# Nine P tiles for six and one buffer of masked keys: P*V put off past the next tile's first score fills in a planned attention and GLU kernel

## The chip, the core and the metric

The kernel runs on one core of a Trainium2 chip. A core has five engines that run side by side, each with its own list of instructions: TensorE (PE in the profile; PEld is its weight load), VectorE (DVE), ScalarE (ACT), GpSimd (POOL) and SyncE (SP, which here only starts transfers). They meet at semaphores. The metric is device time of one execution in microseconds. Before the change it is 268.35 us, the median of three runs (267.51 to 268.49).

## The reference

```python
g = sigmoid((x * gate_w).sum(-1))               # one gate per token, x is [2048, 512]
q, k, v = heads(x @ wq), heads(x @ wk), heads(x @ wv)   # 32 heads of 16, 4 segments of 512 tokens
for s in range(4):
    p     = softmax(q_s k_s^T / 4 + causal mask)
    a_dot = p @ v_s
    a_mem = (phi(q_s) @ M) / (phi(q_s) @ z + 1e-6)       # phi(t) = t + 1 if t > 0 else exp(t)
    o_s   = sigmoid(beta) * a_mem + (1 - sigmoid(beta)) * a_dot
    M += phi(k_s)^T v_s;  z += sum(phi(k_s))
a = concat(o) @ wo
b = (gelu(x @ w_gate) * (x @ w_up)) @ w_down    # 512 -> 1792 -> 512
out = g * a + (1 - g) * b
```

Everything is bfloat16, with sums in float32.

## The kernel before

The program is a list of named tasks. A task is a few instructions on one engine (a few tasks may sit on ACT or DVE). The order of the tasks on each engine is written out in `ORDER` (lines 38 to 136), one string per engine; `schedule` merges the five lists, gives each accumulator of PSUM to the task that comes next, and `Emitter` puts in the semaphore waits that reads and writes of the same buffer need. So an engine's list is kept to the letter, and a task that is not ready holds up all that stand behind it.

The names, with `s` the segment and `t` one of four head tiles (eight heads each):

- `K`, `Q`, `V`: projections, full 128x128 matmuls of 512 columns, two per piece (line 498). Their results are copied out by ACT or DVE (`Kev`, `Qev`, `Vev`).
- `kp`: keys with every other head set to zero, into `kpad` (lines 719 and 728), one buffer for each parity `j`, double by segment before the change. `kl` is the same for the short rows along the diagonal.
- `qk{s}_{t}{A0,B0,L,A1,B1}`: score fills (line 859). Each writes all four score banks `X` with 8 tiled matmuls (`L` with 32). `exp` (ACT, line 866) reads all of `X` at once and writes one P tile `PT[slot]`; `msk` (POOL, line 870) sets the masked part to zero. `X` exists once, so the next fill waits for the exp. There are 72 fills, 64 of them into P tiles, handed out in turn by `pt_next % R_PT`.
- `pv{s}_{t}_{j}`: P*V (lines 909 and 917), 32 tiled matmuls into one accumulator. It reads the P tiles of one tile and parity, which then are free. `pvt` (DVE, line 924) transposes it into `Tb`, `norm` (lines 936 to 944) scales and transposes it back (through `ott`) into `oT`.
- `mz`: the product for M and z, 64 tiled matmuls. `pk`, `pq`: phi of keys and queries (an ACT exp and three DVE instructions); `pkT` and `oTd` are transposing transfers. `num`, `nump`: the memory read.
- `G`, `U`, `D`: gate, up and down projections, full matmuls; `D` ends with the output projection of the attention, which needs `oT`. `gelu` is on ACT, in a block of its own between the exps of two segments; `Um` (DVE, line 1009) multiplies. `fin` scales an output tile into one of `N_OST` buffers, and `out` stores it.

All full matmuls, `num`, `mz` and P*V share four PSUM accumulators `psW`; the next user of one waits until ACT or DVE has read it. What PE does between two score fills is mostly five pieces of two full matmuls; `pv` stands at some places among them.

SP starts the transfers: loads of x, weights, `Vlo` (copies of V rows), `pkT`, `oTd`, `out`, in the order of its list.

Of the kernel before, what the change touches and what calls it, by code (L numbers as in the profile page):

```python
# [17 lines left out]
H = 32  # L18
# [3 lines left out]
P = 128  # L22
ATT_SCALE = 0.25
EPS = 1e-6
R_PT = 6
N_W = 4
N_OST = 3
# [4 lines left out]
PATIENCE = 3.0  # L32
SWITCH = 0.097
COLD = 4.9
HOLD = 0.3
BLOCK, BLOCK_ASK, BLOCK_END = 256, 165, 208
OPEN_BONUS = 6.0
# [3 lines left out]
        "K0_2.0 K0_3.0 K0_0.1 K0_1.1 K0_2.1 K0_3.1 x0t0_1 x0t1_1 K0_0.2 K0_0.3 K0_2.2 K0_3.2 K0_2.3 K0_1.2 "  # L41
        "K0_1.3 K0_1.4 K0_1.5 K0_1.6 K0_1.7 K0_0.4 K0_0.5 K0_0.6 K0_0.7 K0_3.3 K0_2.4 K0_2.5 K0_2.6 K0_3.4 "
        "K0_3.5 Q0_2.0 Q0_1.0 Q0_1.2 Q0_2.2 Q0_3.0 K0_2.7 Q0_3.2 K0_3.6 Q0_0.0 Q0_0.2 K0_3.7 V0_1.0 V0_1.2 "
        "V0_0.0 V0_0.2 qk0_0A0 Q1_2.0 G0_6.0 V0_2.0 G0_6.2 V0_2.2 G0_1.0 qk0_0B0 G0_1.2 Q1_2.2 G0_4.0 G0_4.2 "
        "G1_5.0 G1_5.2 qk0_0L G1_7.0 V0_3.0 V0_3.2 G1_11.0 G1_11.2 G1_7.2 Q1_3.0 qk0_0A1 Q1_3.2 Q1_0.0 Q1_0.2 "
        "Q1_1.0 Q1_1.2 qk0_0B1 G1_3.0 G1_3.2 K1_2.0 G0_8.0 G0_8.2 K1_2.2 qk0_1A0 G1_2.0 G1_10.0 G1_2.2 G1_10.2 "
        "G0_5.0 G0_5.2 qk0_1B0 mz0 pv0_0_1 pv0_0_0 G1_12.0 qk0_1A1 K1_0.0 K1_0.2 G0_11.0 G0_11.2 K1_1.0 K1_1.2 "
        "qk0_1B1 G1_12.2 K1_3.0 K1_3.2 G0_12.0 G0_12.2 G0_10.0 G0_10.2 qk0_2A0 V1_1.0 V1_1.2 G1_4.0 G1_4.2 "
        "G0_9.0 qk0_2B0 pv0_1_1 pv0_1_0 G0_2.0 G0_2.2 G0_9.2 qk0_2L G0_7.0 G0_7.2 G1_6.0 num1_00.0 G1_6.2 G1_8.0 "
        "qk0_2A1 G1_8.2 G1_9.0 G1_9.2 G0_3.0 G0_3.2 qk0_2B1 V1_2.0 num1_01.0 Q2_2.0 V1_2.2 Q2_2.2 num1_02.0 "  # L50
        "qk0_3A0 V1_3.0 Q2_1.0 V1_3.2 G1_13.0 G1_13.2 Q2_1.2 qk0_3B0 pv0_2_0 pv0_2_1 G0_13.0 G0_13.2 num1_11.0 "
        "qk0_3A1 V1_0.0 V1_0.2 G0_0.0 G0_0.2 G1_1.0 G1_1.2 qk0_3B1 pv0_3_0 G1_0.0 G1_0.2 num1_10.0 Q2_3.0 Q2_3.2 "
        "U0_0.0 U0_0.2 qk1_0A0 pv0_3_1 U0_1.0 Q2_0.0 U0_1.2 Q2_0.2 U0_2.0 U0_2.2 U0_7.0 U0_8.0 U0_9.0 U0_9.2 "
        "U0_7.2 U0_8.2 U0_12.0 U0_12.2 U0_4.0 U0_4.2 U0_6.0 U0_6.2 U0_3.0 U0_3.2 U1_2.0 U1_2.2 U1_3.0 U1_3.2 "
        "U0_5.0 U1_5.0 U1_5.2 U0_13.0 U0_5.2 D0_0.0 D0_0.2 U0_13.2 num1_12.0 D0_0.4 D0_0.6 U0_11.0 U0_11.2 "
        "D0_0.8 U0_10.0 qk1_0B0 U0_10.2 D0_2.0 D0_2.2 D0_2.4 D0_2.6 qk1_0L D0_2.8 D0_2.10 D0_2.12 U1_4.0 U1_4.2 "
        "qk1_0A1 U1_0.0 U1_0.2 D0_2.14 D0_0.10 D0_2.16 D0_0.12 qk1_0B1 D0_0.14 U1_11.0 U1_11.2 U1_7.0 U1_7.2 "
        "K2_0.0 qk1_1A0 K2_0.2 U1_12.0 D0_0.16 U1_12.2 U1_10.0 qk1_1B0 U1_1.0 U1_10.2 U1_13.0 U1_1.2 U1_13.2 "
        "qk1_1A1 pv1_0_0 pv1_0_1 mz1 D0_3.0 D0_3.2 qk1_1B1 K2_2.0 D0_3.4 K2_2.2 D0_3.6 D0_3.8 qk1_2A0 V2_0.0 "
        "D0_3.10 pv1_1_0 pv1_1_1 qk1_2B0 D0_3.12 D0_3.14 V2_0.2 D0_3.16 K2_3.0 qk1_2L K2_3.2 D0_1.0 D0_1.2 "  # L60
        "D0_1.4 D0_1.6 qk1_2A1 V2_3.0 V2_3.2 D0_1.8 D0_1.10 U1_6.0 qk1_2B1 D0_1.12 D0_1.14 U1_9.0 U1_6.2 U1_9.2 "
        "qk1_3A0 K2_1.0 K2_1.2 Q3_0.0 Q3_0.2 D0_1.16 qk1_3B0 pv1_2_1 pv1_2_0 U1_8.0 U1_8.2 qk1_3A1 V2_2.0 V2_2.2 "
        "Q3_1.0 Q3_1.2 G2_2.0 qk1_3B1 G2_0.0 G2_0.2 V2_1.0 V2_1.2 G2_2.2 G2_1.0 G2_1.2 G2_3.0 G2_3.2 qk2_0A0 "
        "G2_5.0 G2_4.0 G2_4.2 G2_8.0 G2_8.2 G2_6.0 G2_5.2 G2_7.0 G2_6.2 G2_7.2 pv1_3_0 pv1_3_1 G2_9.0 G2_9.2 "
        "G2_10.0 G2_11.0 G2_10.2 num2_01.0 G2_11.2 G2_12.0 G2_12.2 G2_13.0 G2_13.2 Q3_2.0 Q3_2.2 num2_00.0 "
        "D1_0.0 U2_6.0 num2_02.0 D1_0.2 U2_6.2 D1_0.4 D1_0.6 D1_0.8 qk2_0B0 V3_3.0 D1_0.10 V3_3.2 U2_0.0 U2_0.2 "
        "D1_0.12 D1_0.14 qk2_0L Q3_3.0 Q3_3.2 V3_0.0 V3_0.2 D1_0.16 qk2_0A1 U2_8.0 U2_8.2 U2_13.0 num2_10.0 "
        "U2_13.2 U2_1.0 U2_1.2 qk2_0B1 U2_12.0 num2_11.0 U2_9.0 U2_9.2 D1_2.0 D1_2.2 qk2_1A0 D1_2.4 D1_2.6 "
        "num2_12.0 U2_4.0 U2_4.2 D1_2.8 qk2_1B0 D1_2.10 U2_12.2 D1_2.12 D1_2.14 D1_2.16 qk2_1A1 pv2_0_0 pv2_0_1 "
        "mz2 U2_3.0 U2_3.2 qk2_1B1 U2_10.0 K3_0.0 D1_3.0 K3_0.2 D1_3.2 qk2_2A0 U2_10.2 D1_3.4 K3_2.0 D1_3.6 "  # L70
        "D1_3.8 qk2_2B0 pv2_1_0 pv2_1_1 D1_3.10 D1_3.12 qk2_2L K3_2.2 D1_3.14 D1_3.16 K3_1.0 K3_1.2 qk2_2A1 "
        "V3_1.0 V3_1.2 D1_1.0 D1_1.2 D1_1.4 qk2_2B1 U2_5.0 U2_5.2 D1_1.6 D1_1.8 D1_1.10 qk2_3A0 U2_7.0 D1_1.12 "
        "U2_7.2 U2_11.0 U2_11.2 qk2_3B0 pv2_2_0 pv2_2_1 D1_1.14 D1_1.16 qk2_3A1 V3_2.0 K3_3.0 V3_2.2 K3_3.2 "
        "G3_0.0 qk2_3B1 G3_0.2 U2_2.0 G3_2.0 U2_2.2 G3_1.0 G3_1.2 G3_2.2 qk3_0A0 G3_3.0 G3_3.2 G3_4.0 G3_4.2 "
        "G3_6.0 G3_6.2 G3_5.0 G3_10.0 G3_5.2 G3_10.2 G3_7.0 G3_7.2 G3_9.0 G3_8.0 G3_8.2 G3_9.2 pv2_3_1 pv2_3_0 "
        "G3_11.0 G3_11.2 G3_12.0 G3_12.2 G3_13.0 G3_13.2 U3_12.0 U3_12.2 U3_7.0 U3_7.2 num3_00.0 D2_0.0 D2_0.2 "
# [26 lines left out]
    "dve": (
        "x0ev0a_0 x0ev0b_0 x0ev0_1 K0_1ev kl0_11 K0_0ev kp0_1 kl0_01 kl0_10 K0_2ev kp0_2 kl0_21 gmul0 kp0_0 "
# [101 lines left out]
class Sched:  # L206
# [6 lines left out]
    def add(self, task):  # L213
# [20 lines left out]
        if task.grp is not None:  # L234
            task.grp.left += 1
# [166 lines left out]
def mm_t(n):  # L402
    return max(0.026, n / 2370.0)
# [775 lines left out]
```

## Time and profile before

| | before |
|---|---|
| median of three runs | 268.35 us (267.51 to 268.49) |
| profiled execution, first to last instruction | 265.4 us (its total is not given apart) |
| PE busy | 261.5 us, 3021 matmuls |
| ACT busy | 210.6 us |
| DVE busy | 197.8 us |
| POOL busy | 105.4 us |
| score exp (ACT, line 866) | 72 of 1.88 us |
| granted TensorE clock | 1.00 |
| moved by DMA | 18.23 MB, 69 GB/s on average |

The profile gives one execution. Busy times of engines overlap. The chain of work that ended last is followed back from the last instruction, at each step to what released it or to what stood before it on its engine. A matmul's end in the trace is modelled, so consecutive matmuls overlap in it; from start to start is what one costs.

### The profile page before, as it was taken

Reading aid. Unit: us, or ns where it says so; the run is one execution under the profiler, and the core shown is the slowest. Engines: PE = TensorE matmul, PEld = TensorE weight load, DVE = VectorE, ACT = ScalarE, POOL = GpSimd, SP = SyncE. Lnnn points to the kernel's source line nnn. Section 1 sums busy time; section 2 is a strip of 40 time slices with the busy share of each in tenths; the row PEclk is TensorE's granted clock in tenths of the full one; section 3 lists DMA queues with packets and bytes.
Section 4 is the critical chain, followed back from the end, with each engine's and each line's share of the span. In section 5 each row is a group of like instructions: output and inputs, shape, how many; then the busy total and the mean of one; then the engine's idle time right before and its main releaser. Section 6 shows DMA issues by size and latency. Waiting matters only on the chain.

```text
span 265.4 us, 7149 instructions
## 1 busy us (share of the span) xinstructions
PE 261.5 (99%) x3021; PEld 119.0 (45%) x3021; DVE 197.8 (75%) x389; ACT 210.6 (79%) x187; POOL 105.4 (40%) x256
## 2 busy tenths in 40 slices
PE   8999999999999999999999999999999999999995
PEld 4644444444444435444344444443444444343452
DVE  1789869988988588886768968898685847694651
ACT  3699998999998898897957888867876886767712
POOL 8205777453101357173830161354173071436310
PEclk9999999999999999999999999999999999999999
DMA  7952223429510433200001433200000031300102
GB/s 231 323 161 51 54 82 83 140 42 308 161 51 0 100 77 70 80 0 2 2 0 21 101 84 78 82 2 22 2 2 0 2 78 29 77 22 2 42 0 82
DMA packets 32752, 18.23 MB, mean 69 GB/s; under 512 B 20560, under 2 KB 32720, under 8 KB 32720
## 3 DMA queue, kind: packets, MB, share of 16 engines
q1 hardware_dynamic: 31632, 16.73, 23.4%
q10 hardware_dynamic: 1088, 1.05, 1.1%
q8 instruction: 24, 0.39, 0.6%
q14 instruction: 8, 0.07, 0.1%
HBM read 9.84 MB, written 2.10 MB: 45 GB/s over the span
## 4 chain that ended last, share of the span: by engine, by line
PE 98%; ACT 1%; issue 0%; ACTq 0%
PE psW L498 76%; PE psXALL L859 9%; PE psW L909 6%; PE psXALL L498 3%; PE psW L917 1%; PE psW L583 1%; PE psW L825 1%; ACT pt L866 1%; PE psXALL L591 0%; ACT ost L1038 0%; ACTq L394 0%
## 5 line engine op out<-in xcount | busy, mean ns | idle before, releaser
L866 ACT ACTIVATE pt<-psXALL 128x2048 bf16<-128x2048 f32 x64 | 120.1, 1877 | 25.2 <-PE psXALL L859 20.1
L870 POOL TENSOR_SCALAR_AFFINE_SELECT pt<-pt 128x256 bf16<-128x256 bf16 x128 | 57.1, 455 | 106.7 <-ACT pt L866 102.1
L498 PE MATMUL psW<-xT,wu 128*128 128x512 bf16 x224 | 56.3, 380 | 0.0
L498 PE MATMUL psW<-xT,wg 128*128 128x512 bf16 x224 | 54.2, 380 | 0.0
L498 PE MATMUL psW<-wd,hT 128*128 128x512 bf16 x210 | 53.5, 380 | 0.0
L1009 DVE TENSOR_TENSOR hT<-psW,hT 128x512 bf16<-128x512 f32 x56 | 37.2, 685 | 18.6 <-PE psW L498 18.3
L870 POOL TENSOR_SCALAR_AFFINE_SELECT ptl<-ptl 128x512 bf16<-128x512 bf16 x32 | 23.0, 718 | 32.7 <-ACT ptl L866 31.1
L924 DVE STREAM_TRANSPOSE tb<-psW 128x512 f32<-128x512 f32 x32 | 21.5, 699 | 14.1 <-PE psW L917 14.1
L498 PEld LDWEIGHTS psW<-xT,wg 128*128 128x128 bf16 x224 | 20.4, 98 | 24.3 <-issue 1.5
L498 PEld LDWEIGHTS psW<-xT,wu 128*128 128x128 bf16 x224 | 20.2, 98 | 24.4 <-issue 2.7
L498 PEld LDWEIGHTS psW<-wd,hT 128*128 128x128 bf16 x210 | 19.2, 98 | 22.8 <-issue 2.1
L859 PE MATMUL psXALL<-qT,kpad 32*128 32x320 bf16 (+3 forms) x512 | 25.4, 273 | 0.2 <-ACT pt L866 0.2
L993 ACT ACTIVATE hT<-psW 128x512 bf16<-128x512 f32 x28 | 15.4, 600 | 8.0 <-PE psW L498 8.0
L859 PEld LDWEIGHTS psXALL<-qT,kpad 32*128 32x128 bf16 x512 | 7.6, 92 | 25.8 <-ACT pt L866 16.1
L909 PE MATMUL psW<-pt,vaug 128*17 128x192 bf16 (+3 forms) x512 | 18.8, 273 | 0.0
L866 ACT ACTIVATE ptl<-psXALL 128x2048 bf16<-128x2048 f32 x8 | 15.0, 1877 | 3.7 <-PE psXALL L859 3.7
L498 PE MATMUL psW<-xT,wk 128*128 128x512 bf16 (+1 forms) x80 | 17.8, 337 | 0.0
L498 PE MATMUL psW<-wv,xT 128*128 128x512 bf16 x64 | 17.3, 381 | 0.0
L498 PE MATMUL psW<-wo,oT 128*128 128x512 bf16 x60 | 16.4, 380 | 0.0
L768 POOL COPY exsT<-exs 32x4 f32<-32x4 f32 x64 | 13.4, 209 | 7.2 <-ACT exs L759 3.5
L909 PEld LDWEIGHTS psW<-pt,vaug 128*17 128x17 bf16 x512 | 10.3, 90 | 8.8 <-issue 3.0
L498 PE MATMUL psW<-xT,wq 128*128 128x512 bf16 x48 | 12.8, 380 | 0.0
(101 smaller groups left out, 308.1 us busy)
## 6 DMA issues: line engine op xcount, KB each, us to landing
out_dram<-ost SPq DMA_DIRECT2D x15, 128.0 KB, 1.7
wg<-in_B_w_gate_dram SPq DMA_DIRECT2D x2, 896.0 KB, 7.0
wu<-in_B_w_up_dram SPq DMA_DIRECT2D x2, 896.0 KB, 5.2
wd<-in_B_w_down_dram SPq DMA_DIRECT2D x2, 896.0 KB, 5.9
phkt<-in_A_x_dram SPq DMA_DIRECT2D x3, 512.0 KB, 4.4
vlow<-vaug SPq DMA_DIRECT2D x8, 136.0 KB, 2.6
wk<-in_A_wk_dram ACTq DMA_DIRECT2D x2, 256.0 KB, 4.2
hT<-in_A_x_dram SPq DMA_DIRECT2D x2, 256.0 KB, 3.9
```

The costliest lines, as they stand in the source:

```text
L498: return Instr(lambda e: e.matmul(view(), lhsT, rhs, start=first, stop=last), reads=reads, writes=[fkey if fkey is not None else g.key], e ...
L583: task(f"warm{i}", PE, [Instr(lambda e, gw=gw, n=n: e.matmul(gw.f32()[:, 0:n], ones[:, 0:128], ones[:, 0:n], start=True, stop=True), [], [ ...
L768: cross = task(f"exsT{s}", POOL, [Instr(lambda e, g=g, c=c: e.tensor_copy(exsT[sl][32 * g:32 * g + 32, c:16:4], exs[32 * c:32 * c + 32, s4 ...
L825: Instr(lambda e, t=t, kt=kt, c=c: e.matmul(gm.f32()[32 * c:32 * c + 32, 34 * t:34 * t + 34].rearrange("p (j e) -> p j e", e=17), phkt[:, ...
L859: instrs.append(Instr(lambda e, g=g, lhs=lhs, rhs=rhs, c0=c0, ncol=ncol: e.matmul(X[g][:, c0:c0 + ncol], lhs(32 * g), rhs(32 * g), start=T ...
L866: prev_exp[0] = exp_task(s, f"exp{s}_{t}{name}", [Instr(lambda e: e.activation(dst[:], XALL[:, :].rearrange("p (g c) -> p g c", g=4), ACTF ...
L870: task(f"msk{s}_{t}{name}", POOL, [Instr(lambda e, view=view, pat=pat, base=base: e.affine_select(out=view, in_=view, compare_op=ALU.is_ge ...
L909: instrs.append(Instr(lambda e, t=t, q=q, kb=kb, slot=slot, c0=c0: e.matmul(gp.f32()[32 * q:32 * q + 17, 128 * kb + 64:512], Vaug[sl][:, k ...
L917: instrs.append(Instr(lambda e, t=t, q=q, kb=kb, c0=c0: e.matmul(gp.f32()[32 * q:32 * q + 17, 128 * kb:128 * kb + 64], Vlow[j][:, kb, 4 * ...
L924: task(f"pvt{s}_{t}_{j}", DVE, [Instr(lambda e: e.transpose(Tb[:, j, :], gp.f32()[:, :]), [gp.key], [("Tb", j)], dve_t(512))], grp=gp)
L993: lambda e, g=g, ft=ft, s=s: e.activation(hT[s % 2][:, ft, :], g.f32()[:, :], ACTF.Gelu_apprx_tanh),
L1009: task(f"Um{s}_{ft}", DVE, [Instr(lambda e, g=g, ft=ft: e.tensor_tensor(hT[sl][:, ft, :], g.f32()[:, :], hT[sl][:, ft, :], ALU.mult), [g.k ...
```

## The change

Four things change in the program, and then all five orders are rebuilt.

- `R_PT` goes from 6 to 9: nine P tiles. The memory for them comes from `kpad`, now one buffer per parity instead of two, from `ott`, now the first part of `Tb`, from `gmat`, now `gexp`, and from `N_OST`, 2 output buffers instead of 3.
- `kp` of segments 1 to 3 becomes four tasks of two tiles each (names `kp{s}_{i}{j}`), since a half of `kpad` can be written once the fills of those two tiles are done.
- The P*V tasks stand later in PE's list, past the first fills of the next tile, and some directly between two fills. The most fills that are unread at once are nine.
- Five evacuations of the first x tiles all go to DVE. First use of a score bank by `Q0` is now ordered after the x transposes that used it (`held`). The rest in the planner's classes (`table`, `grps`, `patience`, `ahead`) only names things for the building of orders.

```diff
-R_PT = 6
+R_PT = 9
 N_W = 4
-N_OST = 3
+N_OST = 2
...
-    kpad = [[sb(f"kpad{j}_{i}", [P, 4, 512]) for i in range(2)] for j in range(2)]
+    kpad = [sb(f"kpad{j}", [P, 4, 512]) for j in range(2)]
...
-    ott = sb("ott", [P, 512])
+    ott = Tb.bitcast(BF)[:, 0:1, 0:512].rearrange("p a b -> p (a b)")
...
-    gmat = sb("gmat", [P, H], F32)
+    gmat = gexp
...
+        keys = [key, ("x0ps", 0)] if c0 == 512 else [key]
...
+        held = [("x0ps", c0) for c0 in ((0, 512), (1024,), (2048,), (3072,))[t]] if x else []
...
+        ins[0].writes += tuple(held)
...
         if s > 0:
-            for j in range(2):
-                task(f"kp{s}_{j}", DVE, [
-                    Instr(lambda e, j=j: e.tensor_scalar(kpad[j][sl][:], kT[:], maskc[j][:, 0:1], None, ALU.mult),
-                          [("kT", t) for t in range(4)] + [("c", "mask", j)],
-                          [("kpad", j, sl, t) for t in range(4)], 0.78)])
+            for i in range(2):
+                for j in range(2):
+                    task(f"kp{s}_{i}{j}", DVE, [Instr(lambda e, i=i, j=j: e.tensor_scalar(
+                        kpad[j][:, 2 * i:2 * i + 2, :], kT[:, 2 * i:2 * i + 2, :], maskc[j][:, 0:1], None, ALU.mult),
+                        [("kT", t) for t in (2 * i, 2 * i + 1)] + [("c", "mask", j)],
+                        [("kpad", j, t) for t in (2 * i, 2 * i + 1)], dve_t(1024, 4, ap=True))])
...
-                dst, dk = (oT[sl][:, t, :], ok) if s == 0 else (ott[:], [("ott",)])
+                dst, dk = (oT[sl][:, t, :], ok) if s == 0 else (ott, [("Tb", 0)])
```

PE's order in segment 1, from the third tile's first fill, and the last segment's fills around 225 us, before and after:

```diff
-qk1_1A1 pv1_0_0 pv1_0_1 mz1 D0_3.0 D0_3.2 qk1_1B1 K2_2.0 D0_3.4 K2_2.2 D0_3.6 D0_3.8 qk1_2A0 V2_0.0
-D0_3.10 pv1_1_0 pv1_1_1 qk1_2B0 D0_3.12 D0_3.14 V2_0.2 D0_3.16 K2_3.0 qk1_2L
+qk1_1A1 D0_2.8 num1_12.0 num1_10.0 num1_11.0 D0_2.10 D0_2.12 D0_2.14 qk1_1B1 D0_2.16 U1_12.0 U1_9.0 U1_9.2 U1_12.2
+qk1_2A0 pv1_0_0 pv1_0_1 pv1_1_1 mz1 pv1_1_0 qk1_2B0 D0_1.0 D0_1.2 D0_1.4 D0_1.6 D0_1.8 V2_3.0 qk1_2L
...
-qk2_1A1 pv2_0_0 pv2_0_1 mz2 U2_3.0 U2_3.2 qk2_1B1
+qk2_2A0 mz2 pv2_0_0 pv2_0_1 pv2_1_0 pv2_1_1 qk2_2B0
...
-qk3_1A1 U3_5.0 U3_5.2 num3_12.0 U3_0.0 U3_0.2 qk3_1B1
+qk3_1A1 U3_13.0 num3_11.0 U3_13.2 D2_1.8 D2_1.10 D2_1.12 num3_12.0 qk3_1B1
```

SP's order after the first `pkT`:

```diff
-pkT0_1 Vlo0_0 Vlo0_1 pkT0_2 pkT0_0 pkT0_3 xt1 x2_3 x2_2 x2_1 x2_0 w_wu0 oTd1_1 oTd1_0 w_wu1 w_wd1 w_wo Vlo1_1 w_wd0
+pkT0_0 pkT0_1 Vlo0_0 Vlo0_1 w_wu0 pkT0_3 pkT0_2 x2_3 xt1 w_wd0 w_wu1 x2_0 x2_2 x2_1 w_wd1 w_wo x3_1 oTd1_0 Vlo1_1
```

## The prediction

> **What bounds the kernel now.** I read the busy lines first: which engine has no room, and at what clock.
>
> ```profile
> PE 261.5 (99%) x3021; PEld 119.0 (45%) x3021; DVE 197.8 (75%) x389; ACT 210.6 (79%) x187; POOL 105.4 (40%) x256
> PEclk9999999999999999999999999999999999999999
> PE 98%; ACT 1%; issue 0%; ACTq 0%
> ```
>
> PE is busy 99% of a 265.4 us span, at the full granted clock in every slice, and the chain that ended last runs over PE for 98% of it. A busy PE can hide waits, so I read next the chain in order of time (start, length, what).
>
> ```profile
> 180.93 2.26 PE psW L498 x10
> 191.23 3.13 PE psW L498 x14
> 194.68 7.01 PE psW L498 x32
> ...
> 233.00 0.97 PE psW L498 x4
> 237.80 0.33 PE psXALL L859 x8
> 238.13 2.26 PE psW L498 x10
> 240.39 0.33 PE psXALL L859 x8
> ```
>
> Full matmuls cost 0.216 us each ((7.01-0.97)/28), and each piece has 0.10 to 0.11 us on top (0.97-4*0.216), whatever its length. That is the price of changing between full matmuls and the tiled ones of the score fills (L859) and P*V (L909, L917). Nothing else is in these pieces: PE issues back to back. I laid the start times of all PE instructions beside these prices; only 0.43 us in 261 is left over, and 0.24 of it is one place, in the timeline:
>
> ```profile
> 223.68 0.62 PE L909 MATMUL psW<-pt,vaug 128*17 128x448 bf16 x16
> ...
> 224.24 0.61 PE L909 MATMUL psW<-pt,vaug 128*17 128x448 bf16 x16
> ...
> 224.89 0.40 PE L859 MATMUL psXALL<-qT,kpad 32*128 32x448 bf16 x8
> ...
> 225.48 1.88 ACT L866 ACTIVATE pt<-psXALL 128x2048 bf16<-128x2048 f32 x1 [0.70 <-PE psXALL L859]
> ...
> 227.42 0.40 PE L859 MATMUL psXALL<-qT,kpad 32*128 32x320 bf16 x8 [0.17 <-ACT pt L866]
> ```
>
> Here a fill began at 224.89, its exp ran 225.48 to 227.37, and the next fill, which writes the same score banks, started at 227.42. So a round from fill to fill takes at least 2.53 us by ACT; the usual one (0.33+2.26) takes 2.59 by PE, 0.06 above it. This round had 2.27 us of PE work, and PE waited. The rows also price P*V: the second starts 0.56 us after the first, the fill 0.65 after that, so leaving P*V costs 0.09 to 0.10 as well, also towards a fill.
>
> The waits view says how near the others are:
>
> ```profile
> ACT pt L866 <- PE psXALL L859: 20.1, 38, 1.1
> PEld psXALL L859 <- ACT pt L866: 17.8, 42, 0.7
> DVE hT L1009 <- PE psW L498: 18.3, 25, 2.9
> PEld psW L498 <- DVE otok L800: 0.6, 3, 0.2
> ```
>
> ACT and DVE wait for PE; the weight loads' waits on ACT run under the preceding matmuls.
>
> **The change part by part.** No PE instruction is added or removed: 3021 before and after. What can move PE is its mode changes, its waits and the two ends.
>
> *Mode changes.* Counted along both PE orders, neighbours of different kind go from 165 to 159: full to tiled 75 to 71, P*V (or memory product) to full 15 to 9, P*V to fill 3 to 7, fill to P*V 12 to 10, fill to full 60 to 62. By the rows above each costs 0.10, towards a fill too: -6*0.10 = -0.6 us. Placing P*V between fills saves only the return to full matmuls, which is why the gain is not larger.
>
> *The wait at 225.4.* Adding up the new order's PE work from fill to fill with the rows' prices, that round now holds 2.91 us. Before, one round held 2.27 and ten 2.48 to 2.51; after, four hold 2.48 to 2.50. The wait goes: -0.24. The six fewer short rounds are worth at most 6*0.04 = 0.2 and the left-over is 0.19, so I take -0.1.
>
> *ACT work between exps.* Exp is 1.88 of the 2.53, so another ACT instruction of up to 0.65 (copies of 0.60, a 0.62 sum) fits a round free; a phi exp of 1.05 does not. The tightest place: phi exp and copy in two successive rounds, 1.88+1.05+1.88+0.60 = 5.41 of ACT in 5.53 of PE. It fits. If one such round fails it costs 0.1 to 0.4. I take 0, range 0 to 0.4.
>
> *P*V put off.* With nine P tiles up to nine fills stay unread: P*V of tiles 0 and 1 of the second segment follows the ninth. Each P*V drags two DVE transposes (0.70 each) and the normalisation (recip, scales, transpose, sum: about 2.6) with it; behind them on DVE stand the U products that free PE's four accumulators, and the output projection waits for the result. Cover: DVE idles 67 us in all, but the tightest place has none to spare: the projection piece of segment 2 that needs the last normalisation lies 5.5 us of PE work after its P*V begins, and P*V pair 1.2, 0.3 to the transpose (224.24 to 224.55 in the timeline), a transpose 0.70, a U product 0.69 that stands between, and normalisation 2.6 make 5.5. Accumulators change hands with less spare than before in more places, too. Before, loads waited about 1.4 us in total on DVE and none of it reached PE; bounds 0 to 1.4, I take +0.1, nearest to what reached PE.
>
> *One buffer of masked keys.* Per segment two 128x2048 scalings (0.78 each, six in all) become four of 128x1024. Rows: 128x512 takes 0.35, 128x2048 0.78, so about 0.49; DVE gains 3*(4*0.49-2*0.78) = 1.2 us, inside its idle time. The new wait is on the previous segment's fills of the same two tiles; each half stands in DVE's list after those fills, so what is queued behind it (U products) does not stall. 0; if one is late, a U product of 0.69 is late with it, 0 to 0.7.
>
> *Transposed result in Tb, gate matrix in the exponentials' place.* Readers and writers are on DVE in this order already, or long done: 0. *x0 score banks held:* the first Q matmul in each starts at 8.64 or later, the last x evacuation ended at 7.14: 0. All five evacuations of x go to DVE: the last then ends at 6.75+0.43 = 7.18, and its first reader starts at 7.33: 0, at most 0.1.
>
> *Two output buffers.* The last copy now waits for the landing of tile 1's store. From the end of tile 1's work to the last matmul's end the order holds 3.4 us of PE work; copy 0.75, landing 1.7 and 0.3 between make 2.75. 0; with the transposes' landing of 2.4 it would be just even.
>
> *SP order.* Three weight loads (wu0, wd0, wu1) move ahead of pieces of the next x. The nearest row: two such loads, issued at 58.9 and 59.5, landed at 63.9 and 66.3. Issued after the memory product at about 45, behind 512 KB of tokens, they land by about 53; the x transposes behind them by about 54. The Q matmul that reads them is at 56.8 on the new order. wg's second half is issued at 12.0, landed at 17.9 and is now read at 19.1 instead of 20.6. 0; 0 to 1.0 if a landing slips.
>
> *Instruction fetch.* The page shows no cost, only the queue:
>
> ```profile
> q8 instruction: 24, 0.39, 0.6%
> ```
>
> 24 packets for 6042 weight loads and matmuls: one per 256, that is per 128 matmuls. Densest before: memory product and one P*V pair, 128 matmuls; P*V pairs of two tiles and the memory product now form runs of 192, 2.87 us, in two places (segments 1 and 2). Within them 128 matmuls take 1.9 us. The trace's packets took 0.88 to 1.40 us and began at least 5.7 us apart. If asking and landing take the 1.6 us of the shortest row of transfers, nothing is lost; at the transposes' 2.4 to 2.8, 0.5 to 0.9 in each place. I take 0, the nearest case being the dense runs before, none of which stalled; range 0 to 1.8.
>
> [...]
>
> **Sum**: -0.6 - 0.24 - 0.1 + 0.1 = -0.84 us against the profiled execution, whose span is 265.4; 2.95 us of the median lie outside it and are untouched (the execution's own total is not given apart). 268.35 - 0.85 = 267.5 us, -0.3%. Three runs of before spread over 0.98 us, so 0.5% (1.34 us) is about what a measurement tells from no change.
>
> **The rivals.**
> *Nothing gets in the way and the small left-overs vanish too.* -0.6-0.43-0.1 = about -1.15, 267.2, and a median as low as before's lowest run against its median gives 266.4: faster by over 0.5%. For it: PE has hardly any wait left. Against: it needs luck in the runs.
> *The gain is given back on ACT or DVE.* PE's freed 0.1s fall in rounds 0.06 above ACT's floor, and accumulators are tighter. For it: 42 of the fills' weight loads waited on ACT. Against: those waits were hidden. Gives back 0.4 to 0.8: 268.1.
> *Slower: instruction fetch in the two runs of 192.* It decides from the point where two stalls exceed 0.84, a landing of 2.3 us; slower by over 0.5% from 0.84+1.34 = 2.18 in two places, a landing of 3.0. At 3.3 us it costs 2*1.4: 270.3. For it: the 512 KB token load is issued as the memory product ends, and those rows land in 4.4. Against: packets took 1.4 at most beside other traffic.
> *Slower by a late transfer*, x behind the weights: +1.0 to +2.5, about 269.
>
> **How the numbers follow.** Forecast 0.52 (own range 267.0 to 268.0), left-overs and luck 0.23, given back 0.12, fetch 0.08, late transfer 0.05. Faster by over 0.5%: 0.23 and 0.03 of the forecast's edge, 0.26. Slower: fetch and half of the late transfer, 0.11. Same: 0.63. The range leaves out the fetch and the low end of the luck: 266.5 to 269.2.
>
> **What would show it.** Right: PE work from first to last matmul shorter by 0.6 to 1.1 us, no wait at a fill over 0.1, P*V followed by a fill in seven places at 0.65 start to start. Wrong: a gap inside the runs of P*V and memory product with no releaser (fetch); weight loads waiting on DMA before a Q matmul; fills over 2.6 us apart with ACT as releaser.

## The result, and the profile after

The changed kernel takes 270.10 us (median of six executions, 269.42 to 273.52); the kernel before, run beside it and earlier, 267.67 us (six, 267.26 to 268.49). The ratio is 1.0087 with a 95% interval of 1.0058 to 1.0116: slower by 0.87%, where 0.3% faster was forecast and the range ended at 269.2. The slowest of the six, 273.52, ran at a mean granted clock of 0.994 and is not in the ratio, nor are the slowest execution of `e1_split` (275.79) and of `e5_shift48` (276.0) below; without it the median is 269.94. The profiled execution took 270.25 us, its span is 268.5 us; before's was 265.4.

The page of the kernel after, first the busy time of the engines, then the queue that brings the instructions (packets, MB, share) and the chain that ended last by engine:

```profile
PE 262.4 (98%) x3021; PEld 119.2 (44%) x3021; DVE 202.2 (75%) x399; ACT 210.5 (78%) x180; POOL 105.1 (39%) x256
...
q8 instruction: 23, 0.38, 0.6%
...
PE 90%; DMA 5%; SPq 2%; ACT 1%; issue 1%; ACTq 1%
```

PE's share of the chain fell from 98% to 90%, although PE has the same 3021 matmuls. What has come in is DMA and SP's queue, where the chain runs back through a transfer that PE waited for, and 1% "issue", time that nothing in the profile explains. The waits view of PE (engine, line, what it waited for: us in total, times, longest) names them:

```profile
PE psXALL L860 <- issue: 1.3, 1, 1.3
...
PE psW L497 <- DMA xT<-in_A_x_dram: 0.5, 1, 0.5
PE psXALL L497 <- DMA wq<-in_A_wq_dram: 0.4, 1, 0.4
```

The timeline of PE around 109 us shows the largest (start, length, instruction, idle time before it):

```profile
105.30 0.40 PE L860 MATMUL psXALL<-qT,kpad 32*128 32x448 bf16 x8
105.63 0.61 PE L908 MATMUL psW<-pt,vaug 128*17 128x448 bf16 x16
...
107.52 0.81 PE L828 MATMUL psW<-vaug,phkt 128*32 128x34 bf16 x64
...
108.83 0.31 PE L860 MATMUL psXALL<-qT,kpad 32*128 32x320 bf16 x3
110.42 0.39 PE L860 MATMUL psXALL<-qT,kpad 32*128 32x320 bf16 x5 [1.28 <-issue]
```

This is the run `qk1_2A0 pv1_0 pv1_1 mz1 qk1_2B0` that the prediction priced. PE stops in the middle of one fill, with three of its eight matmuls done. No semaphore can stand there: the other five read and write the same buffers. From start to start the stop costs 1.58 us. A second one, 0.31 us, follows the same run in segment 2 (the chain, followed in order of time, has "174.89 0.15 issue" there).

The chain in order of time shows the second loss:

```profile
50.30 3.20 SPq L524
...
53.55 4.78 DMA xT<-in_A_x_dram
58.33 0.05 issue
58.38 0.82 PE psW L497 x3
```

The transposing load of a quarter of x for segment 2 is issued at 53.55 and lands at 58.33; the second matmul of `Q2_2` waits for it: 0.65 us from start to start.

The place around 225 us that the prediction gave 0.24 for is clean. The two rounds that begin with the exps below are 2.89 us (227.02 to 229.91) and 2.6 us long, and ACT waits for PE, not PE for ACT (ACT's timeline; in brackets ACT's idle time and what ended it):

```profile
227.02 1.88 ACT L866 ACTIVATE pt<-psXALL 128x2048 bf16<-128x2048 f32 x1 [0.96 <-PE psXALL L860]
229.91 1.88 ACT L866 ACTIVATE pt<-psXALL 128x2048 bf16<-128x2048 f32 x1 [1.01 <-PE psXALL L860]
```

I laid all PE start times of the two traces beside the same price for each kind of piece and neighbour. PE's work went from 260.32 to 259.70 us, PE's waits (what is over those prices) from 0.55 to 4.30. The terms of the 3.16 us between the two spans:

| term | predicted | in the two profiles |
|---|---|---|
| mode changes, 165 to 159 | -0.6 | -0.62 |
| wait at 225.4 | -0.24 | -0.24 |
| instruction fetch, two runs | 0 | +1.58 + 0.31 |
| SP order, x behind weights | 0 | +0.65 |
| P*V put off, accumulators | +0.1 | +0.20 |
| a fill that waits for an exp, at 47.7 | 0 | +0.09 |
| small left-overs, shorter rounds | -0.1 | none found |
| two output buffers | 0 | +0.21 |
| the head: warm-up matmuls, load of wq | not in the sum | +0.4 + 0.60 |

The last row is not the change's. The warm-up matmuls ran at 0.43 us each until 3.4 us in before's profile and until 4.5 in the one after, and wq's second half landed at 9.27 and at 10.45, from the same list of transfers. In the kernels below with the head of after the wait for wq was 0 to 0.22, and `e7_bmodes`, whose head is that of before to the instruction, also did its first transposes at 4.85 us, not 4.34. The first transposes in before, in after and in `e7_bmodes` (PE's timelines):

```profile
4.34 0.62 PE L591 MATMUL psXALL<-ident,hT 128*128 128x128 bf16 x8
4.75 0.61 PE L591 MATMUL psXALL<-ident,hT 128*128 128x128 bf16 x8
4.85 1.06 PE L591 MATMUL psXALL<-ident,hT 128*128 128x128 bf16 x8
```

So before's one profile had a fast start. Without the last row the terms add up to 2.18, and the medians differ by 2.27 (269.94 less 267.67), not by 3.16.

### The profile page after: what moved, and what is told of

The parts are those of the page before. It is cut to its first block, busy times and chain, and to the rows that moved or that the text cites. A ratio compares the mean times of both kernels' runs of the same rounds, so it can differ in the third digit from the quotient of the medians.

```text
span 268.5 us, 7155 instructions
## 1 busy us (share of the span) xinstructions
PE 262.4 (98%) x3021; PEld 119.2 (44%) x3021; DVE 202.2 (75%) x399; ACT 210.5 (78%) x180; POOL 105.1 (39%) x256
## 3 DMA queue, kind: packets, MB, share of 16 engines
q10 hardware_dynamic: 1088, 1.05, 1.2%
## 4 chain that ended last, share of the span: by engine, by line
PE 90%; DMA 5%; SPq 2%; ACT 1%; issue 1%; ACTq 1%
PE psW L497 71%; PE psXALL L860 9%; PE psW L908 6%; DMA wq<-in_A_wq_dram 3%; PE psXALL L497 3%; DMA xT<-in_A_x_dram 2%; SPq L524 2%; PE psW L916 1%; ACT ptl L866 1%; ACTq L528 1%; PE psW L828 0%; SPq L528 0%; ACT ost L1036 0%; ACT hT L511 0%; ACTq L393 0%
## 5 line engine op out<-in xcount | busy, mean ns | idle before, releaser
L869 POOL TENSOR_SCALAR_AFFINE_SELECT pt<-pt 128x256 bf16<-128x256 bf16 x128 | 55.3, 443 | 111.9 <-ACT pt L866 107.0
L497 PE MATMUL psW<-wd,hT 128*128 128x512 bf16 x210 | 55.3, 380 | 0.0
L869 POOL TENSOR_SCALAR_AFFINE_SELECT ptl<-ptl 128x512 bf16<-128x512 bf16 x32 | 23.9, 746 | 29.1 <-ACT ptl L866 27.4
L497 PEld LDWEIGHTS psW<-wd,hT 128*128 128x128 bf16 x210 | 18.4, 98 | 21.2 <-issue 2.7
L771 POOL COPY exsT<-exs 32x4 f32<-32x4 f32 x64 | 15.4, 240 | 8.2 <-ACT exs L762 4.6
L497 PE MATMUL psW<-wv,xT 128*128 128x512 bf16 x64 | 18.1, 380 | 0.0
L514 DVE CAST hT<-psW 128x512 bf16<-128x512 f32 x20 | 13.5, 686 | 4.3 <-PE psW L497 4.3
```

The costliest lines, as they stand in the source:

```text
L497: return Instr(lambda e: e.matmul(view(), lhsT, rhs, start=first, stop=last), reads=reads, writes=[fkey if fkey is not None else g.key], e ...
L514: alts[DVE] = [Instr(lambda e: e.tensor_copy(dst(), src()), reads=reads, writes=writes, est=dve_t(n))]
L771: cross = task(f"exsT{s}", POOL, [Instr(lambda e, g=g, c=c: e.tensor_copy(exsT[sl][32 * g:32 * g + 32, c:16:4], exs[32 * c:32 * c + 32, s4 ...
L869: task(f"msk{s}_{t}{name}", POOL, [Instr(lambda e, view=view, pat=pat, base=base: e.affine_select(out=view, in_=view, compare_op=ALU.is_ge ...
```

## The experiments

### The two runs broken up, x first, and both

`e1_split` puts the second P*V pair behind full matmuls in both runs. `e2_xfirst` gives SP the x quarters ahead of the weights. `e3_both` has both edits.

```diff
 PE, e1_split
-qk1_2A0 pv1_0_0 pv1_0_1 pv1_1_1 mz1 pv1_1_0 qk1_2B0 D0_1.0 D0_1.2 ... D0_1.8 V2_3.0 qk1_2L
+qk1_2A0 pv1_0_0 pv1_0_1 mz1 D0_1.0 qk1_2B0 D0_1.2 ... D0_1.8 V2_3.0 pv1_1_1 pv1_1_0 qk1_2L
-qk2_2A0 mz2 pv2_0_0 pv2_0_1 pv2_1_0 pv2_1_1 qk2_2B0 D1_3.0 D1_1.0 ... D1_1.6 qk2_2L
+qk2_2A0 mz2 pv2_0_0 pv2_0_1 D1_3.0 qk2_2B0 D1_1.0 ... D1_1.6 pv2_1_0 pv2_1_1 qk2_2L
 SP, e2_xfirst
-x2_3 xt1 w_wd0 w_wu1 x2_0 x2_2 x2_1
+x2_3 x2_0 x2_2 x2_1 xt1 w_wd0 w_wu1
```

> The changed kernel with two edits of PE's order, all else kept: in segment 1 the second P*V pair (pv1_1) moves from inside the run qk1_2A0 .. qk1_2B0 to just ahead of qk1_2L, behind five full-size pieces, and one D piece goes between mz1 and qk1_2B0; in segment 2 the same with pv2_1 and mz2. The work is the same; the two runs of 192 small matmuls are broken into 144 or fewer with full-size pieces between. Theory A, instruction fetch: PE takes its instructions in blocks of 256 (128 matmuls with their weight loads), the next block but one is only asked for when a block is entered, and a block of small matmuls is through in 1.9 us (109 us) and 3.9 us (175 us, its stall within) while the ask takes about 3.5. With full-size pieces in it the block lasts over 4.5 us. Expected: the stall of 1.58 us at 109 and the one of about 0.3 to 0.5 us at 175 are gone, four more mode changes cost 0.4; time 270.1 - 1.9 + 0.4 = 268.6 us (268.2 to 269.0). Rival B, a late P tile, mask or PSUM bank at these two places that the profile does not name: the fill qk1_2B0 stands in the same place behind the same exponentials, so it stalls as before (1.3 to 1.6 us) and the time is 270.3 to 270.7 us.

> The changed kernel with one edit of SP's order: the last three quarters of x for segment 2 (x2_0, x2_2, x2_1) are issued ahead of xt1 and the two weight pieces w_wd0 and w_wu1, as far as before had them ahead. Theory: the wait of Q2_2.2 for x2_1 at 58.4 us (0.65 us with the slow start behind it) goes, since x2_1 lands about 8 us earlier; the weight pieces land by about 58 and are first read near 63 (U1) and 85 (D0), the gate input xt1 is read by DVE only near 60. Expected 270.1 - 0.6 = 269.5 us (269.2 to 269.8), the two stalls at 109 and 175 unchanged at 1.6 and 0.3 to 0.5 us. Rival: the wait is not on the path, because PE then waits as long a little later (for U weights or DVE): the 0.65 us are gone at 58 and come back before 70, 270.1 us.

> The edits of e1_split and e2_xfirst together. If the two stalls of instruction fetch and the wait for x2_1 are separate terms, they add: 270.1 - 1.9 + 0.4 - 0.6 = 268.0 us (267.5 to 268.5), level with the kernel before (267.67). If the gains overlap or the time is lost again somewhere else, over 268.6 us. If something beyond these two makes the changed kernel slow (more work on PE by the new order, contention of ACT or DVE), it stays above 269 us.

Measured against before (267.85 us in these runs): `e1_split` 269.29 us (269.08 without its slowest execution), ratio 1.0043 (1.0019 to 1.0068); `e2_xfirst` 269.24 us, 1.0047 (1.0016 to 1.0078); `e3_both` 268.66 us, 1.0022 (1.0003 to 1.0040).

In `e1_split` both stops are gone from PE's waits. PE's work grew by 0.44 us for four more mode changes, as expected. The time came out 0.5 over the expectation, and PE's timeline says where part of it is:

```profile
107.57 0.60 PE L498 MATMUL psW<-wo,oT 128*128 128x512 bf16 x2
108.61 0.40 PE L861 MATMUL psXALL<-qT,kpad 32*128 32x320 bf16 x8 [0.44 <-ACT pt L867]
```

The fill `qk1_2B0`, now earlier, waits 0.52 us for an exp (start to start; 0.44 as the view counts). `mz1` before it waits 0.22, and the two waits for x, which this kernel keeps, were 1.07 in its profile instead of 0.65. This is ACT at that time:

```profile
106.10 0.69 ACT L1054 ACTIVATE ost<-psW,omgt 128x512 bf16<-128x512 f32 x1 [1.02 <-DMA out_dram<-ost]
106.69 1.87 ACT L867 ACTIVATE pt<-psXALL 128x2048 bf16<-128x2048 f32 x1
```

ACT stood for 1.02 us, because the copy of output tile 2 goes into the buffer of tile 0, whose store had not landed. The exp stands behind that copy in ACT's list. `mz1` starts 0.15 us after the copy ends, which frees an accumulator. The kernel after has the same wait (1.1 us), and there `pv1_1_1` pays 0.21 us (start to start) for that accumulator:

```profile
106.22 0.69 ACT L1053 ACTIVATE ost<-psW,omgt 128x512 bf16<-128x512 f32 x1 [1.11 <-DMA out_dram<-ost]
106.96 0.43 PEld L908 LDWEIGHTS psW<-pt,vaug 128*17 128x17 bf16 x16 [0.17 <-ACT ost L1053]
```

Before, with three output buffers, no copy waits for a store. The link is read from the waits; a kernel with another assignment of buffers to tiles was not run, so it is not shown by an experiment.

In `e2_xfirst` the four matmuls of `Q2_2` run through:

```profile
57.26 1.03 PE L498 MATMUL psW<-xT,wq 128*128 128x512 bf16 x4
58.22 0.40 PE L861 MATMUL psXALL<-qT,kpad 32*128 32x448 bf16 x8
```

x2_1 lands at 46.69 instead of 58.33, and the 0.65 us do not come back elsewhere; the stop at 109 us is still 1.59 us. So the late transfer is a term of its own. The stop of 0.31 at 175 shrank to 0.02 in this execution: the instruction packet there took 1.18 us instead of 1.43. In `e3_both` neither loss is left; what remains over the 268.0 expected are, by its profile, the waits behind ACT's late copy, 0.52 and 0.29 us.

### The same order, moved in the blocks

If PE's instructions come in blocks, what counts is where a block begins, not which fill stands there. `e4_shift` keeps order, buffers and work, and makes 104 matmuls more at the head out of the same columns.

```diff
+        nw = 4 if n == 512 else 1                      # warm-up: 512 columns as 4 x 128
...
+        nv = 4 if x else nu                            # K0: 256 columns as 2 x 128, Q0: 512 as 4 x 128
+        sub = [[slice(c.start + v * (c.stop - c.start) // nv, c.start + (v + 1) * (c.stop - c.start) // nv)
+                for v in range(nv)] for c in cols]
```

> The changed kernel with its order and work kept, only 104 matmuls more in the first 13 us: eight 512-column warm-up matmuls are made as four of 128 columns, the 256-column K0 matmuls as two of 128, the 512-column Q0 matmuls as four of 128. That moves every later instruction by 208 places in PE's blocks of 256 and changes nothing of data, buffers or order. Theory A, instruction fetch: a stall sits where one block is all small matmuls, so the stalls move: at 109 and 175 us the blocks then last 4.3 to 4.5 us and the stalls of 1.58 and 0.3 to 0.5 go; at about 45 us (the run pv0_1 qk0_2L mz0) the block then lasts 1.9 to 2.2 us where it lasted 5.2, and a new stall of 1.2 to 1.7 us stands there. Net 270.1 - 1.9 + 1.5 = 269.7 plus 0 to 1.0 for the smaller matmuls of the head. Rival B, a late P tile, mask or PSUM bank: the stalls stay at 109 and 175 at 1.6 and 0.3 to 0.5 us, nothing new stands at 45, and the time is 270.1 plus the head's 0 to 1.0.

Measured: 268.36 us, ratio 1.0012 (0.9987 to 1.0036). The stops at 109 and 175 are gone, with nothing touched behind the head. That a late P tile, mask or bank caused them is ruled out. PE's timeline at the old place:

```profile
107.80 0.40 PE L864 MATMUL psXALL<-qT,kpad 32*128 32x320 bf16 x8
108.13 1.04 PE L497 MATMUL psW<-wo,oT 128*128 128x512 bf16 x4
```

But the new stop expected at 45 us did not come, although the block there is as dense (1.69 us). Its successor's packet had begun 0.83 us before TensorE entered the block; at 109 us in the kernel after it began 1.00 us behind the entry. So the first version of the theory missed something, and two more kernels were made to see what.

`e5_shift48` has 24 matmuls more (the warm-up alone); `e8_shift48x` is the same with the SP order of `e2_xfirst`; `e9_shift144x` has 72 more, also with that SP order.

```diff
 e5, e8
+        nw = 4 if n == 512 else 1
 e9
+        nw = 4 if n == 512 else 1
+        nv = 2 if x else nu
```

> The changed kernel with its order and work kept, only 24 matmuls more at the head: the eight 512-column warm-up matmuls are made as four of 128 columns. That moves every later instruction by 48 places in PE's blocks of 256. In e4_shift 104 matmuls more took the stall at 109 us away and no new one came at 45, where a block is all small matmuls too (1.85 us) but is entered straight behind full-size pieces: its successor's packet began 0.64 us before TensorE entered the block, at 109 us it began 0.8 to 1.0 us after. Theory A2: the ask goes out when PE's sequencer enters a block; it is ahead of TensorE behind full-size pieces and not behind small ones. With 24 more the block at 109 is entered 51 small matmuls into the run and the one at 175 some 50 into it, and both blocks hold nothing but small matmuls (1.85 and 2.2 us). Expected: 1.4 to 1.7 us of stall at about 108.5, and 1.0 to 1.4 at 174 where the changed kernel has 0.3 to 0.5: 0.5 to 1.0 us slower than the changed kernel, 270.6 to 271.2 us. Rival: the stall hangs on which buffer or mask is late, and e4_shift moved it by the slightly different times of its head; then the stalls stay 1.58 and 0.3, time 270.1.

> The kernel of e5_shift48 (24 matmuls more at the head, every later instruction moved by 48 places in the blocks of 256) with the SP order of e2_xfirst, so that the wait for x2_1, which was 2 us in the one profile of e5_shift48, is out of the way. Theory A2 (the ask for the next block but one goes out when PE's sequencer enters a block, and the sequencer is not ahead of TensorE among small matmuls): the blocks at 108 and 174 us are entered some 50 small matmuls into a run and hold nothing but small ones, so stalls of 1.4 to 2.2 us at 108 to 113 and of 0.6 to 1.4 at 175 to 179. Against e2_xfirst (269.24 us, stalls of 1.59 and 0) that is 0.5 to 1.5 us more: 269.8 to 270.8 us. Rival: the place in the blocks does not matter beyond the head; stalls 1.59 and 0, 269.2 us.

> The same with 72 matmuls more at the head (warm-up in pieces of 128 columns, K0 in pieces of 128, Q0 in pieces of 256), so every later instruction is moved by 144 places; order, work and buffers of e2_xfirst. Now the three densest blocks are entered right where a run of small matmuls begins (at about 44, 105 and 170 us), behind full-size pieces, and are all small matmuls, 1.8 to 2.6 us long. Theory A2: the sequencer is ahead of TensorE there, the ask goes out some 0.6 us before TensorE enters the block, the packet lands before or just as it is needed: stalls of 0 to 0.4 us at each of the three, time about that of e6_best, 268.0 us (267.6 to 268.8). Theory A1, as the first experiments put it (the ask goes out when TensorE itself enters the block and takes 3.5 us): stalls of 0.9 to 1.7 us at each, together 3 to 4.5 us, 271 to 272.5 us.

Measured: `e5_shift48` 273.21 us (272.01 without its slowest execution), 1.0159 (1.0105 to 1.0212); `e8_shift48x` 271.51 us, 1.0121 (1.0081 to 1.0161); `e9_shift144x` 271.49 us, 1.0144 (1.0107 to 1.0181). Of `e5_shift48` only the places of the stops are used, since the clock fell within its profiled execution (see the end). The time of `e8_shift48x` missed its range upwards too: the profiled execution, with the clock at 1.00 throughout, took 269.93 us, the other three, at 0.993 to 0.994, 271.39 to 272.25. In PE's timeline of `e8_shift48x`:

```profile
106.53 0.59 PE L910 MATMUL psW<-pt,vaug 128*17 128x448 bf16 x11
108.28 0.25 PE L910 MATMUL psW<-pt,vaug 128*17 128x192 bf16 x4 [1.16 <-issue]
...
171.70 0.21 PE L918 MATMUL psW<-ptl,vlow 128*17 128x64 bf16 x3
173.50 0.28 PE L918 MATMUL psW<-ptl,vlow 128*17 128x64 bf16 x13 [1.59 <-issue]
```

and of `e9_shift144x`:

```profile
47.33 0.36 PE L865 MATMUL psXALL<-qT,kpad 32*128 32x448 bf16 x1
48.26 0.40 PE L865 MATMUL psXALL<-qT,kpad 32*128 32x448 bf16 x7 [0.57 <-issue]
...
107.28 0.38 PE L833 MATMUL psW<-vaug,phkt 128*32 128x34 bf16 x27
109.13 0.46 PE L833 MATMUL psW<-vaug,phkt 128*32 128x34 bf16 x37 [1.47 <-issue]
```

PE now stops in the middle of a P*V, of a memory product and of another fill. Counted from the program's first matmul, the stops stand after the same numbers of matmuls, whichever kernel has one: 1238 in after, `e2_xfirst`, `e5_shift48`, `e8_shift48x` and `e9_shift144x`; 2002 or 2003 in after, `e5_shift48`, `e8_shift48x` and `e9_shift144x`; 602 in `e9_shift144x` and in `e10_shift156x` below. These are 636 and 764 or 765 apart, five and six times 128 less three or four. With its weight load each matmul is two instructions, and before's 24 packets of q8 for 6042 of them make about 252 a packet; the distances of the stops make 254 to 255, near the 256 of the theory. So the program's count says where a stop can stand, whatever code is there; whether one came differed with the block ahead of it and with the start of the packet (in the table below a block of 1.69 us whose packet began 0.83 us early had none, one of 1.76 us whose packet began 0.50 us late had 1.42). That settles the cause.

`e9_shift144x` was also to decide how the ask is timed, and the version written down as A2 fell: three stops of 0.93, 1.54 and 1.35 us came where it had 0 to 0.4, and the time lies in the range of A1. One reason was left, a wait ahead of the block's first instruction. `e10_shift156x` moves everything by six matmuls more, so that the block of the run at 105 us is entered two matmuls ahead of its first fill:

```diff
-        nw = 4 if n == 512 else 1
+        nw = n // 128
```

> The kernel of e9_shift144x with six matmuls more at the head (the three 384-column warm-up matmuls made as three of 128), so every later instruction is moved by 12 places more. In e9_shift144x the block of the first dense run was entered by the fourth matmul of qk1_2A0 at 105.24 us; this fill waits for an exp that ended at 105.04, and the packet began at 106.78, 1.7 us after that. Theory A3: the ask goes out when PE's sequencer comes to the block's first instruction, and a semaphore wait ahead of it, here that of the fill on the exp, holds the sequencer back. Now the block is entered two matmuls ahead of the fill, in U1_9.2, ahead of that wait. Expected: the packet begins 0.7 to 2 us earlier against the fill, and the stall in the run falls from 1.54 to 0 to 0.7 us; the block at 172, entered by the sixth matmul of its fill as before behind the fill's wait, keeps 1.2 to 1.6 us, and the one at 47 keeps 0.6 to 1.0. Time 271.5 - 1.1 = 270.4 us. Rival A1 (the ask goes out when TensorE itself enters the block): six matmuls are 0.6 us at most, the stall falls to 0.9 to 1.4.

Measured: 271.24 us, 1.0127 (1.0070 to 1.0184). Entry, packet and stop in the densest blocks, read from the traces (the entry is TensorE's start of the matmul 128 before the place of the stop; us):

| kernel | block entered at, matmul of the small run | packet began after the entry | block lasted | stop |
|---|---|---|---|---|
| after | 106.97, 76th | +1.00 | 1.87 | 1.58 |
| after | 171.70, 84th | +0.62 | 2.81 | 0.31 |
| `e2_xfirst` | 105.90, 76th | +0.75 | 1.87 | 1.59 |
| `e8_shift48x` | 105.11, 52nd | +0.50 | 1.76 | 1.42 |
| `e8_shift48x` | 169.37, 60th | +1.18 | 2.35 | 1.78 |
| `e9_shift144x` | 44.34, 40th | +1.05 | 2.99 | 0.93 |
| `e9_shift144x` | 105.24, 4th | +1.54 | 2.23 | 1.54 |
| `e9_shift144x` | 170.45, 12th | +0.73 | 1.70 | 1.35 |
| `e10_shift156x` | 44.86, 34th | +1.24 | 1.70 | 1.53 |
| `e10_shift156x` | 105.71, ahead of it | -0.78 | 3.29 | 0 |
| `e10_shift156x` | 170.34, 6th | -0.82 | 1.80 | 0 |
| `e4_shift` | 43.86, 8th | -0.83 | 1.69 | 0 |

At 105 us the stop went and the packet began 2.3 us earlier against the entry, as A3 had it. That the block is also longer there (a mask or accumulator wait of 0.35 and the full matmuls ahead) would have left A1 a stop of 0 to 0.8 (3.2 to 4.1 us, the time from entry to the next block's first matmul at the stops, less 3.29), so this one place does not part the two well. The control failed: the stop at 172 us was to stay and went, because that packet also began early, before the exp ended that its fill waits for. So A3 as written, a wait that holds the ask back, does not hold. What the table does show: entered ahead of a run or among its first eight small matmuls, the packet began 0.8 us early in three cases of four; entered deeper in the run it began 0.5 to 1.2 us late, in every case.

The other blocks of the traces say the same with less regularity. Of 234 blocks in the profiles of all kernels but `e5_shift48`, from 14 us on, 93 are entered more than ten small matmuls into a run, and in each of them the packet began after the entry, by 0.9 us in the median. Of the other 141 it began ahead of the entry in 93: in 60 of 76 where other transfers took under 0.1 of the DMA engines' time in the microsecond before the entry, in 21 of 46 where they took over 0.4. At the entry of `e9_shift144x` at 105.24 they took 0.71. So other traffic is a rival for what made that packet late by 1.54; no run changes it by itself, and the question stays open.

All this is one profiled execution of each kernel. That of `e10_shift156x`, with one stop left, took 269.69 us; the other four, at a clock of 1.00 too, took 270.6 to 271.95, and the median of 271.24 lies over the 270.4 expected and level with `e9_shift144x`. So the places that were entered early there may well stop in other executions.

### What a mode change costs

`e7_bmodes` is the kernel before with 20 mode changes more, and nothing else.

```diff
-pv0_1_1 pv0_1_0 G0_2.0
+pv0_1_1 G0_2.0 pv0_1_0
...
-pv1_0_0 pv1_0_1 mz1 D0_3.0
+pv1_0_0 pv1_0_1 D0_3.0 mz1
```

> The kernel before with ten changes of PE's order: eight P*V pairs and two runs of P*V and memory update have one full-size piece put between their parts instead of behind them, so that PE goes 185 times from one tiling of the array to another instead of 165; work, buffers and all other orders are kept. If a change costs the 0.10 us that the prediction took, PE's work grows by 20 x 0.10 = 2.0 us and the time to 267.85 + 2.0 = 269.9 us (269.6 to 270.2). Rival: a change costs nothing by itself and the start-to-start differences stand for something else; 267.9 us. Its head is that of before to the instruction: if the warm-up of before (first transpose at 4.34 us against 4.75 to 4.85 in five kernels of the new order) is a matter of the run, this one can show 4.8 as well.

Measured: 270.38 us against 268.20, ratio 1.0088 (1.0064 to 1.0112); 2.18 us more, where 2.0 was expected. PE's work by start times went from 260.32 to 262.26 us: 1.94 for 20 changes, 0.097 each. Its rows show it in one place: P*V to full matmul and back, 0.54 us for the piece of two matmuls (126.05 to 126.59) that takes 0.43 among its own kind.

```profile
126.05 0.61 PE L498 MATMUL psW<-xT,wu 128*128 128x512 bf16 x2
126.59 0.61 PE L909 MATMUL psW<-pt,vaug 128*17 128x448 bf16 x16
127.03 0.29 PE L917 MATMUL psW<-ptl,vlow 128*17 128x64 bf16 x16
127.25 0.60 PE L498 MATMUL psW<-xT,wu 128*128 128x512 bf16 x2
```

### Both losses out without a mode change

`e6_best` is `e4_shift` with the SP order of `e2_xfirst`.

> e4_shift (104 matmuls more at the head, order and work kept) with the SP order of e2_xfirst. Neither the stalls at 109 and 175 us nor the wait for x2_1 at 58 is left, and no mode change is added. From the trace of e4_shift (268.36 us) only what x2 costs in its other runs is taken away, 0 to 0.6: 267.9 us (267.4 to 268.4), level with or 0.2 us better than the kernel before; if the mode changes saved (0.6 us) were all of the difference, 267.3. Rival: something else in the new order costs 0.5 us in most runs, and it stays at 268.4 or above.

Measured: 268.05 us (twelve executions, 266.90 to 269.59) against 268.20 for before in the same runs; ratio 0.9995 (0.9973 to 1.0018). This takes back what the change had cost and is level with before; by the interval it is at most 0.7 us better or 0.5 worse. Whether the mode changes saved make a shorter time is thus not shown: they stand in the profiles' sum alone. Its page:

```profile
PE 261.4 (99%) x3125; PEld 123.7 (47%) x3125; DVE 202.0 (76%) x399; ACT 210.4 (79%) x180; POOL 105.5 (40%) x256
...
PE 99%; ACT 0%; issue 0%; ACTq 0%
```

## Why the prediction was wrong, point by point

- **Mode changes, right.** -0.62 on PE for six fewer, and 0.097 each when 20 were put into the kernel before.
- **The wait at 225.4, right.** It is gone; one other fill waits 0.09 us for an exp, at 47.7.
- **ACT between exps, masked keys, matrix places, x evacuations at 0, right.** But for those 0.09 none of them ends a wait of PE.
- **Small left-overs at -0.1, not seen.** The rows of the table leave no room for such a gain.
- **P*V put off, size nearly right.** +0.1 was taken; a piece that waits for an accumulator at about 28 us costs 0.20 in the profiles of the new order. The planner's estimated times choose which accumulator a task gets, and `table` changed them as well, so this wait need not come from the order alone.
- **Instruction fetch, the step that failed.** The sum put 0 because "the nearest case" was "the dense runs before, none of which stalled". By the boundaries found here the shortest blocks of before lasted 3.7 and 4.9 us, those of after 1.87 and 2.81. Before has a stretch of 128 matmuls of 1.69 us too, at 32.7 us, but it is spread over two blocks, and the dense runs share their blocks with full matmuls: they were no near case, and where the blocks fall was not looked at. The rival's arithmetic was sound: it counted 1.9 us for 128 small matmuls and said that 2.3 us from asking to landing decides. The size was wrong: from the entry of a block to the first matmul of the next it took 3.2 to 4.1 us at the stops, of which the packet is 0.9 to 1.5 and the time from its landing to that matmul 1.2 to 1.5. The prediction took the landing for the end of it. It also took a packet to be asked for as the block ahead is entered, an assumption that no trace shows; at the dense blocks packets began from 0.8 us before that entry to 1.5 us after it. With 3.4 us it would have had 1.5 and 0.6. The other 20 of 22 blocks in the profile of after lasted 4.1 us or more, and PE did not stop behind them. The chance of 0.08 was too small for a term whose upper bound, 1.8, nothing in the trace excluded. The kernel's own planner (`BLOCK` and `fetched` in `schedule`) counts PE's instructions in blocks too, with times that are assumptions of the code, no measurements; the prediction did not use it.
- **SP order, the second step that failed.** "They land by about 53; the x transposes behind them by about 54" was an estimate from a row in which two weight loads stood alone. After, with 512 KB of tokens ahead of them, w_wd0 landed at 54.4, w_wu1 at 56.7, and x2_1, issued at 53.5 after an issue of 3.2 us for the quarter ahead of it, at 58.33. The row 0 to 1.0 held it, at 0.65; the value taken was 0.
- **Two output buffers, mis-sized.** The term was put at 0. Only the last copy at the end of the kernel was looked at. The trace has the wait in segment 0, where tiles 0 and 2 follow each other: 1.1 us on ACT, 0.21 on PE, and 0.7 to 0.8 in `e1_split` and `e3_both`, as read from the waits.
- **The base of the sum.** The 2.95 us said to lie outside the profiled execution mix two things: in the execution after, time and span differ by 1.75 (270.25 less 268.5), so before's profiled execution was itself about 1.2 us under the median. The forecast difference does not hang on it.
- **As a whole.** The two larger terms that make the kernel faster, -0.6 and -0.24, were right to the tenth in the profiles. Three terms set to zero cost 2.75 us together, and the gap with no releaser and the Q matmul that waits for a transfer are two of the signs that the prediction had named for being wrong. They were taken as mishaps with small chances each; but all came with the same act, pulling work closer together and giving up slack, and for two of them the prediction's own ranges went to 1.8 and 1.0.

## What to carry to other kernels

When a change packs small matmuls together, count PE's instructions in the blocks that the packets and stops show (here 252 to 255, so nearly 128 matmuls with their weight loads) and ask how long each block lasts: here a block entered deep among small matmuls had to last 3.2 to 4.1 us, and one of 128 small ones lasted 1.7 to 2.4. Moving the whole stream by 104 matmuls (`e4_shift`), or full matmuls between the small ones (`e1_split`), took the stop of 1.58 us away; the former added no mode change, but with 24 matmuls more (`e8_shift48x`) PE stopped for 1.42 and 1.78 us, so a later change of the program can bring the stops back. A term that is set to zero by the nearest row needs that row to be near in the thing that matters, and transfers that are moved behind large loads have to be counted in bytes, one after the other: x2_1 landed at 58.33 behind them and at 46.69 ahead of them.

## What the runs showed of the hardware that was not expected

- PE did not go on when the packet had landed: at nine stops it went on 1.2 to 1.5 us after the landing (in the kernel after 108.89 and 110.42). The stops have no releaser in the profile; they show as "issue" in the middle of a group of matmuls (1.28 us there).
- The packet did not begin at one fixed place of TensorE: at the dense blocks it began 0.8 us before TensorE entered the block or up to 1.5 us after, and after it in all 93 blocks where more than ten small matmuls stood in front, by 0.9 us in the median.
- In one profile the clock fell behind two gaps of PE of 2.4 and 2.1 us. That execution, of `e5_shift48`, had a mean granted clock of 0.988, and its windows (busy us of PE, PEld, DVE, ACT and POOL, then the granted clock, the DMA share and GB/s) show it at 0.57 and 0.58 behind them; full matmuls start 0.43 us apart there, not 0.22:

```profile
58.00:60.00 2.00, 0.06 (x1) 0.00 (x0) 1.51 (x3) 0.53 (x2) 1.51 (x4) 1.00 0.47 123
60.00:64.00 4.00, 3.94 (x18) 1.21 (x19) 0.25 (x1) 1.81 (x2) 0.00 (x0) 0.57 0.54 171
...
112.00:114.00 2.00, 0.38 (x25) 0.32 (x29) 1.90 (x6) 0.00 (x0) 0.00 (x0) 1.00 0.29 66
114.00:118.00 4.00, 4.00 (x19) 1.48 (x19) 2.33 (x4) 2.82 (x2) 1.38 (x4) 0.58 0.47 137
```

Behind stops of 1.4 to 1.8 us in the profile of `e8_shift48x` the clock stayed at 1.00. The other three executions of that kernel, which had a mean clock of 0.993 or 0.994, took 1.5 to 2.3 us longer; they have no profile. That a gap of about 2 us is what lowers the clock was seen in one profile and not tested by itself.
